# A sequence DFT with odd rows folded once more and even rows sorted by s mod 8

## The chip, the cores and the metric

The kernel runs on one core of a Trainium2 chip. The metric is device time in microseconds, as the median of several runs. TensorE (PE) multiplies matrices into PSUM banks, VectorE (DVE) and ScalarE (ACT) work on SBUF and PSUM, GpSimd (POOL) works on SBUF and issues gathers, and SyncE (SP) issues most of the plain loads and stores. Each engine takes its instructions in the order of the program.

## The reference

What is computed is a Fourier mixing of 8 batches of 3008 x 256 numbers, of which the real part is kept, followed by two dense layers with an ELU between them:

```python
X = np.fft.fft(x, axis=1)
X = np.fft.fft(X, axis=2)
x = X.real.astype(np.float32).reshape(8 * 3008, 256)
h = x @ w_in                        # 256 -> 2048
g = np.where(h > 0.0, h, np.exp(np.minimum(h, 0.0)) - 1.0)
return (g @ w_out).astype(np.float32)   # 2048 -> 256
```

## The kernel before

All matrices are float32. The channel DFT is folded into the first weights once (`fold_chunk`: `Wc` and `Ws` are w_in behind a cosine and a sine transform), so that the sequence DFT of a batch needs only a cosine part R and a sine part I, each of 128 rows (channels) and 1504 + 1 wave numbers; k and 3008 - k share them. `Rr`, `Ir` and `Rb` are rings of 2048 columns (`RING`), which hold R, I and one spread-out row, the transform of channel 128, for all 8 batches one after another. A tile is 256 columns (`TW`), and 47 tiles of 8 slots, each of two blocks of 128 of the 2048 inner channels, give 376 slots.

A slot, by its names in the schedule: P (`mm_P`, Wc x Rr into a PSUM bank `H`), V (`even_part`, adds the spread row to it, gives `E`), Q (`mm_Q`, adds Ws x Ir to `H`), h (`h_minus`, 2E - H, the mirrored wave numbers), b+ and b- (ReLU of the negative on ScalarE), x+ and x- (exponentials), g+ and g- (the ELU, VectorE, into `G`). From tile 2 on the second layer runs as a Winograd product, with four block sums per slot on POOL (`sum_1`, `sum_3`, `sum_2`, `sum_4`) and seven products (X1, X2, X3) on TensorE; `comb_*` and `turn_*` (tiles u, v, ot) put the result together on VectorE, and SP stores it. There are three banks `H`, shared with the DFTs.

The sequence DFT of a batch. `load_x` brings 4 tiles `xl0` to `xl3` of 128 x 6 rows: rows s of the first quarter, and their mirrors 3008 - s, 1504 - s and 1504 + s. Six rows stand on a partition p: rows 4p to 4p + 3 and 508 + 2p + m. Tiles 0 and 3 come by plain DMAs on SP (`ahead`), tiles 1 and 2, whose rows run backwards, by gathers on POOL (`back`) with row numbers from `row_tables`. `fold_x` folds the channels (`e`, `o`) and then the mirrored rows, so that four tiles of 6 x 128 columns remain: EO0 to EO3, for R and I, even and odd wave numbers (`kodd`). In the first batch VectorE folds (the hand-written list `FRONT`, whose times order the program at the start), in later ones POOL does, a piece per slot.

Each of the four transforms (`Dft`) has three products for even rows and three for odd rows (`dft_parts`, called through `dft_mms` and `Dft.mms`, recorded at line 430), with a folded tile as the stationary matrix and a cosine or sine table `MC[ri, kodd]` as the moving one. The even half gives symmetric and antisymmetric columns: ScalarE copies one part (`copy`, tile `anti`), VectorE adds and subtracts (`unfold`, tile `bs`); `plus` and `minus` then join even and odd rows and write k and its mirror into the ring. The times of later transforms are given by `at_dft`: matmuls at 4.75 in a slot, copy, unfold and join in the next one. `T = 4.8` is the unit of the schedule; events are sorted by time, which is the order of the program, and each engine follows it as its operands come. `load_ext`, `get_ext`, `fold_ext`, `dft_ext`, `ext_*` do the same for channel 128 of batches 1 to 7; `x_even` and `dft_ext_0` for batch 0.

Of the kernel before, what the change touches and what calls it, by code (L numbers as in the profile page):

```python
# [9 lines left out]
FP = mybir.dt.float32  # L10
# [17 lines left out]
NH = 189  # L28
BE = 4 * NH
BW = BE + 3 * NE  # L30
# [3 lines left out]

def _dft_consts():

    p = np.arange(128)[:, None]
    out = np.zeros((128, 4, BW), np.float64)
    for ri in range(2):
        fn = np.cos if ri == 0 else np.sin
        for kodd in range(2):
            mat = out[:, 2 * ri + kodd]
            n, h = (NO, NO // 2) if kodd else (NE, NH)

            def block(m, n):  # L50
                k = 2 * np.arange(n)[None, :] + kodd
                s = 4 * p + m if m < 4 else 508 + 2 * p + m
                w = np.where(s == 0, 0.5, 1.0) * (s <= RUN)
                w = np.where(s == RUN, 0.5 if ri == kodd else 0.0, w)
                return s, w * fn(2.0 * np.pi * ((s * k) % SEQ) / SEQ)

            for m in (0, 2, 4):
                s, v = block(m, h)
                anti = (s % 4 == 2) != ri
                if not kodd:  # L60
                    v[:, h - 1] *= ~anti[:, 0]
                if m < 4:
                    c = 0 if m == 2 * ri else h
                    mat[:, c : c + h] = v
                else:
                    mat[:, 2 * h : 3 * h] = v * ~anti
                    mat[:, 3 * h : 4 * h] = v * anti
            for t in range(3):
                mat[:, BE + t * NE : BE + t * NE + n] = block(2 * t + 1, n)[1]
    return out.reshape(128, -1).astype(np.float32)  # L70
# [34 lines left out]

@with_exitstack
def kernel(
# [31 lines left out]
    def xrows(b, row, step, n, rows=6):  # L139

        return bass.AP(
            tensor=xt,
            offset=x.offset + (b * SEQ + row) * ND,
            ap=[[step * ND, n], [1, rows * ND]],
        )
# [3 lines left out]
    ix = cpool.tile([128, 3], I32, tag="ix")  # L149

    def row_tables():

        for c, n, base, step in (
            (0, 128, HALF - 3, -4),
            (1, 128, HALF - 513, -2),
            (2, 128, HALF - 3, -4),
            (2, 1, HALF - 4, 0),
# [3 lines left out]
                    ix[0:n, c : c + 1],  # L163
                    pattern=[[0, 1]],
                    base=base,
                    channel_multiplier=step,
                )
            )

    def load_x(b):  # L170
# [6 lines left out]
        def back(j, few):  # L177
            cols = slice(0, 2 * ND) if few else slice(2 * ND, 6 * ND)
            c = 1 if few else 2 if j == 1 and b == NB - 1 else 0
            pin(  # L180
                nc.gpsimd.indirect_dma_start(
                    out=L[j][:, cols],
# [5 lines left out]
                    element_offset=(b * SEQ + (HALF if j == 1 else 0)) * ND,  # L188
                )
            )  # L190
            if b == NB - 1 and j == 1 and not few:
                nc.gpsimd.dma_start(
                    out=L[1][0:1, 2 * ND : 5 * ND], in_=xrows(b, SEQ - 3, 1, 1, 3)
                )

        def ahead(j, row):
            nc.sync.dma_start(out=L[j][:, 0 : 4 * ND], in_=xrows(b, row, 4, 128, 4))
            nc.sync.dma_start(
                out=L[j][:, 4 * ND :], in_=xrows(b, row + 512, 2, 128, 2)
            )  # L200

        loads = [lambda n=n: back(2 - n // 2, n % 2) for n in range(4)]
        return L, loads + [lambda: ahead(3, HALF), lambda: ahead(0, 0)]


# [186 lines left out]
    for kodd in range(2):  # L392
        for ri in range(2):
            MC[ri, kodd] = cpool.tile(
                [128, BW], FP, tag=f"MC{ri}{kodd}", name=f"MC{ri}{kodd}"
            )

    def load_mats(ri, kodd, cuts=()):
        n = (2 * ri + kodd) * BW
        ends = (0, *cuts, BW)  # L400
# [120 lines left out]
    def fold_x(L, engine_of, cuts_of):  # L521
# [45 lines left out]
        return [E[1], E[3], O[1], O[3]], ops  # L567
# [961 lines left out]
```

## Time and profile before

| | |
|---|---|
| median of 3 runs | 1944.76 us (1944.68 to 1945.83) |
| span of the profiled execution | 1943.2 us |
| instructions in it | 26993 |
| matmul passes on TensorE | 8912 |
| granted TensorE clock | 1.000 |
| SP queue's DMAs, share of 16 engines | 14.8% |

The profile comes from one execution; its span is the time from the first to the last instruction, and the median is 1.6 us above it. In lines of instructions, `H<-MC,o` reads: the tile written, then the tiles read; line numbers are those of the listing, and L430, L436, L439, L442 and L527 are helpers that record all matmuls, the VectorE and POOL sums, the ScalarE operations and the folds. A float32 product appears as two passes.

### The profile page before, as it was taken

The page shows a single profiled execution, that of the slowest core. Times are in us where ns is not written, and L with a number is a line of the kernel's source. Part 1 is how long each engine was busy: PE and PEld are TensorE (multiplying, and loading weights), DVE is VectorE, ACT ScalarE, POOL GpSimd, SP SyncE. Part 2 cuts the span into 40 slices and gives each one's busy share as a digit, 9 for nine tenths or more (in the row PEclk, how much of TensorE's full clock was granted, in tenths as well). Part 3 has the DMA queues.
Part 4 walks back from the last instruction along what each step waited for, and adds up shares of the span by engine and source line. Part 5 has one row for each costly group of instructions (what it writes and reads, how often), then busy time and mean ns, then how long its engine had stood idle before and what let it go on. Part 6 is the DMA issues. An engine that isn't in the chain of part 4 may idle for free.

```text
span 1943.2 us, 26993 instructions
## 1 busy us (share of the span) xinstructions
PE 1933.4 (99%) x8912; PEld 1653.4 (85%) x8912; DVE 1293.2 (67%) x2398; ACT 865.6 (45%) x1671; POOL 1377.6 (71%) x1816
## 2 busy tenths in 40 slices
PE   9999999999999999999999999999999999999999
PEld 6788788888888888888888888888888888888887
DVE  8866666666666666666667666676666766667666
ACT  5644434443444444444444443444434444344443
POOL 4788758876677767787677876777767776556655
PEclk9999999999999999999999999999999999999999
DMA  8145111101112020020210202012020110100101
GB/s 333 44 35 52 34 44 19 49 15 33 33 20 49 12 50 21 18 50 11 54 23 13 52 8 58 12 20 60 7 52 11 20 23 14 17 12 11 23 11 23
DMA packets 263291, 70.25 MB, mean 36 GB/s; under 512 B 248607, under 2 KB 249523, under 8 KB 263153
## 3 DMA queue, kind: packets, MB, share of 16 engines
q1 hardware_dynamic: 257360, 55.69, 14.8%
q0 software_dynamic: 3616, 12.59, 2.1%
q8 instruction: 70, 1.15, 0.2%
q14 instruction: 69, 0.56, 0.1%
q10 hardware_dynamic: 2176, 0.26, 0.1%
HBM read 43.66 MB, written 24.80 MB: 35 GB/s over the span
## 4 chain that ended last, share of the span: by engine, by line
PE 94%; DVE 2%; POOL 2%; ACT 1%; DMA 1%; issue 1%; DVEq 0%; POOLq 0%
PE H L430 38%; PE pB L430 16%; PE pC L430 16%; PE pD L430 16%; PE pA L430 8%; DMA xl<-in_x_dram,ix 1%; POOL WT L439 1%; POOL G L439 1%; DVE G L869 0%; DVE E L839 0%; DVE e L527 0%; POOL w L439 0%; DVE v L436 0%; ACT G L442 0%; DVE pow L310 0%
## 5 line engine op out<-in xcount | busy, mean ns | idle before, releaser
L439 POOL TENSOR_TENSOR G<-G 128x256 f32<-128x256 f32 x1440 | 1036.8, 730 | 508.5 <-DVE G L869 338.6
L839 DVE SCALAR_TENSOR_TENSOR E<-Rb,wex,H 128x256 f32<-128x256 f32 x752 | 327.7, 477 | 544.7 <-PE H L430 541.1
L442 ACT ACTIVATE G<-H 128x512 f32<-128x512 f32 x376 | 224.6, 597 | 960.1 <-DVE G L853 955.4
L430 PE MATMUL H<-Ir,Ws 128*128 128x256 f32 x1504 | 386.9, 380 | 2.0 <-DVE E L839 2.0
L430 PE MATMUL H<-Rr,Wc 128*128 128x256 f32 x1504 | 387.0, 380 | 0.8 <-DVE Ir L436 0.8
L430 PE MATMUL pC<-G,WT 128*128 128x256 f32 x1440 | 369.5, 379 | 0.0
L430 PEld LDWEIGHTS H<-Rr,Wc 128*128 128x128 f32 x1504 | 284.6, 190 | 56.0 <-issue 2.2
L430 PEld LDWEIGHTS H<-Ir,Ws 128*128 128x128 f32 x1504 | 278.8, 189 | 49.6 <-DVE E L839 4.3
L430 PEld LDWEIGHTS pC<-G,WT 128*128 128x128 f32 x1440 | 273.6, 190 | 37.2
L853 DVE SCALAR_TENSOR_TENSOR G<-E,H 128x512 f32<-128x512 f32 x376 | 256.8, 683 | 44.2 <-POOL G L439 5.0
L869 DVE SCALAR_TENSOR_TENSOR G<-G,H 128x512 f32<-128x512 f32 x376 | 255.8, 680 | 43.0 <-ACT G L442 43.0
L869 DVE SCALAR_TENSOR_TENSOR G<-M,G 128x512 f32<-128x512 f32 x376 | 256.7, 683 | 0.4 <-ACT M L442 0.4
L442 ACT ACTIVATE G<-G 128x512 f32<-128x512 f32 x376 | 233.2, 620 | 0.0
L430 PE MATMUL pD<-G,w 128*128 128x256 f32 x784 | 229.4, 379 | 0.5 <-POOL G L439 0.5
L430 PE MATMUL pA<-G,w 128*128 128x256 f32 x784 | 229.3, 379 | 0.0
L430 PE MATMUL pB<-G,w 128*128 128x256 f32 x784 | 229.3, 379 | 0.0
L442 ACT ACTIVATE M<-G 128x512 f32<-128x512 f32 x376 | 224.0, 596 | 3.1 <-DVE G L853 3.1
L442 ACT ACTIVATE M<-M 128x512 f32<-128x512 f32 x376 | 221.0, 588 | 0.1
L430 PE MATMUL pB<-G,WT 128*128 128x256 f32 x720 | 214.8, 380 | 0.3
L430 PE MATMUL pD<-G,WT 128*128 128x256 f32 x720 | 214.1, 379 | 0.0
L430 PEld LDWEIGHTS pD<-G,w 128*128 128x128 f32 x784 | 148.9, 190 | 21.1 <-POOL G L439 0.9
L430 PEld LDWEIGHTS pA<-G,w 128*128 128x128 f32 x784 | 149.0, 190 | 20.5
(148 smaller groups left out, 1408.2 us busy)
## 6 DMA issues: line engine op xcount, KB each, us to landing
out_dram<-ot SPq DMA_DIRECT2D x496, 32.0 KB
xl<-in_x_dram SPq DMA_DIRECT2D x16, 512.0 KB
xl<-in_x_dram SPq DMA_DIRECT2D x16, 256.0 KB
out_dram<-ot SPq DMA_DIRECT2D x256, 2.0 KB
Rb<-r SPq DMA_DIRECT2D x10, 376.0 KB
raw<-in_moe_w_in_dram SPq DMA_DIRECT2D x7, 512.0 KB
MC<-dft_mats SPq DMA_DIRECT2D x3, 943.5 KB
raw<-in_moe_w_out_dram SPq DMA_DIRECT2D x4, 512.0 KB
```

Source lines behind the costliest of these rows:

```text
L430: nc.tensor.matmul(out_, lhsT=lhsT, rhs=rhs, start=start, stop=stop, skip_group_check=True)
L439: pin(nc.gpsimd.tensor_tensor(out=o, in0=a, in1=b, op=op))
L442: pin(nc.scalar.activation(out=o, in_=i, func=func, **kw))
L839: nc.vector.scalar_tensor_tensor(out=S.E[:, c], in0=Rb[:, cols(i)], scalar=wex[:, f : f + 1], in1=S.H[:, c], op0=ALU.mult, op1=ALU.add,)
L853: nc.vector.scalar_tensor_tensor(out=two(S.G[:, 0:512])[:, :, ::-1], in0=two(S.E), scalar=2.0, in1=two(S.H), op0=ALU.mult, op1=ALU.subtract,)
L869: nc.vector.scalar_tensor_tensor(out=o, in0=e, scalar=-1.0, in1=h, op0=ALU.add, op1=ALU.max)
```

## The change

Odd rows of even wave numbers: since a row s and its mirror 752 - s have the same cosine up to the sign that k / 2 decides, the sum S and the difference D of two of the three odd-row column groups are formed once per batch (S0, D0 from EO0; S2, D2 from EO2), and wave numbers 4j and 4j + 2 take only one of them each. Even rows: they are ordered so that a column group has only s = 0 mod 8, s = 4 mod 8 or s = 2 mod 4, and a product runs over a quarter (95 or 94) or a half (189 or 188) of the wave numbers. The tables have 1417 columns for even and 1786 for odd wave numbers, instead of 1887 each.

In return `unfold` has four operations instead of two, joins of even wave numbers go in two halves with a step of two columns, and the rows of `x` need another order: pairs of rows with steps of 8. Each of the 4 tiles is now loaded in 3 pairs, 6 of the 12 pairs by gathers (one each) and 6 by two plain DMAs each. At the start the six gathers and the plain loads of tile 3 (SP) come first, then those of tiles 2, 0 and 1 on the ACT queue, ahead of ScalarE's table load; `w1_chunks[0].load()` on SP comes behind tile 3. The element-wise loads of channel 128 are cut accordingly, into 24 steps. In later batches the six gathers are spread over the same time as the four before.

```diff
-NH = 189
-BE = 4 * NH
-BW = BE + 3 * NE
+NA = (95, 94)
+NC = (189, 188)
+BW = (1417, 1786)
+OFF = (0, 1417, 3203, 4620)
...
+RUNS = (
+    (0, 0, 96, 0, 8),
+    (0, 96, 128, 500, 8),
+    (1, 0, 94, 750, -8),
+    (1, 94, 128, 266, -8),
+    (2, 0, 64, 4, 8),
+    (2, 64, 128, 258, 8),
+)
...
+        def gather(j, pair):
+            back = j in (1, 2)
+            cut = b == NB - 1 and j == 1 and pair == 0
+            c = 3 if cut else pair
+            block = 2 - pair if back else pair
...
+        def runs(j, queue=nc.sync):
+            back = j in (1, 2)
+            for pair, p, q, r, step in RUNS:
+                if back != (pair == 1):
+                    continue
+                row = (0, SEQ, HALF, HALF)[j] + (-r - 1 if back else r)
+                queue.dma_start(
+                    out=L[j][p:q, 2 * pair * ND : (2 * pair + 2) * ND],
+                    in_=xrows(b, row, 8, q - p),
+                )
+
+        loads = [
+            lambda j=j, pair=pair: gather(j, pair)
+            for j, pair in ((3, 1), (2, 0), (2, 2), (0, 1), (1, 0), (1, 2))
+        ]
+        loads += [lambda j=j, **kw: runs(j, **kw) for j in (3, 2, 0, 1)]
...
+        for n, t in ((0, E[1]), (2, O[1])):
+            d = spool.tile([128, 256], FP, tag=f"sd{n}", bufs=1, name=f"sd{n}")
+            sd.append(d)
+            for m, f in ((0, ALU.add), (1, ALU.subtract)):
+                op(f"{'SD'[m]}{n}", d[:, 128 * m : 128 * m + 128],
+                    t[:, 128:256], t[:, 384:512], f)
...
-        if par:
-            n = NO if kodd else NE
-            return [(2 * t + 1, BE + t * NE, n, 0) for t in range(3)]
-        h = NO // 2 if kodd else NH
-        return [(2 * ri, 0, h, 0), (2 - 2 * ri, h, h, h), (4, 2 * h, 2 * h, 0)]
+        na, nc_ = NA[kodd], NC[kodd]
+        if not par:
+            return [
+                (0, 0, 2 * na, 0),
+                (2, 2 * na, nc_, 2 * na),
+                (4, 2 * na + nc_, na + nc_, na),
+            ]
+        z = 3 * na + 2 * nc_
+        if kodd:
+            return [(2 * t + 1, z + t * NO, NO, 0) for t in range(3)]
+        n = (188, 189) if ri else (189, 188)
+        return [
+            (6, z, n[0], 189 if ri else 0),
+            (7, z + n[0], n[1], 0 if ri else 189),
+            (5, z + NE, NE, 0),
+        ]
...
-        h, m = (n + 1) // 2, n // 2
-        tt(o[0:M, 0:h], sym[0:M, 0:h], anti[0:M, 0:h], ALU.add)
-        tt(o[0:M, n - 1 : n - 1 - m : -1], sym[0:M, 0:m], anti[0:M, 0:m], ALU.subtract)
+        tt(ab[:, 0:na], a, b, ALU.add)
+        p, q = (b, a) if ri else (a, b)
+        tt(ab[:, steps_of(nc_ - 1, 94, -1)], p[:, 0:94], q[:, 0:94], ALU.subtract)
+        tt(es[0:M, 0:nc_], ab[:, 0:nc_], c, ALU.add)
+        p, q = (c, ab) if ri else (ab, c)
+        tt(es[0:M, steps_of(n - 1, 188, -1)], p[:, 0:188], q[:, 0:188], ALU.subtract)
...
-    exp_neg(warm)
-    L_first, loads = load_x(0)
-    for load in loads[:5]:
-        load()
+    L_first, loads = load_x(0)
+    for load in loads[:7]:
+        load()
+    for load in loads[7:]:
+        load(queue=nc.scalar)
+    exp_neg(warm)
     w1_chunks[0].load()
-    loads[5]()
...
-        (-8.58, "E0 Ws0 EO0"),
+        (-8.58, "E0 Ws0 EO0 S0 D0"),
-        (-5.76, "w1b EO2"),
+        (-5.76, "w1b EO2 S2 D2"),
-        (24.53, "u2p w4R Xa3 V5 b-4 u3l"),
+        (24.53, "u2p w4R Xa3 V5 b-4 u3l L4"),
-        (32.25, "u3s L3 Q6 w4P g-5 Xb4 b+6 h6 J-up u3M"),
+        (32.25, "u3s L3 L5 Q6 w4P g-5 Xb4 b+6 h6 J-up u3M"),
...
-    for n in range(16):
-        j, k = divmod(n, 4)
+    for n in range(24):
         at(
-            (14.4 + 0.5 * n) * T,
-            lambda j=j, k=k: load_ext(j, 192 * k, 192 * (k + 1)),
+            (14.4 + 0.33 * n) * T,
+            lambda n=n: load_ext(*divmod(n, 6)),
         )
...
-        for n in range(6):
-            t = l0 + gap * n if n < 4 else l0
+        for n in range(10):
+            t = l0 + gap * n / 1.5 if n < 6 else l0
```

`ab`, a new tile of 189 columns, holds the inner sum of `unfold`; `near` takes the place of `anti`, with 95 columns. Each `load_ext` step is two DMAs, one for each row of a pair.

## The prediction

> **What bounds the kernel now.** I read the page first (busy times, chain), then the busy times by stage, then TensorE and VectorE in order of time around two transforms in the middle, then the first 30 us.
>
> ```profile
> PE 1933.4 (99%) x8912; PEld 1653.4 (85%) x8912; DVE 1293.2 (67%) x2398; ACT 865.6 (45%) x1671; POOL 1377.6 (71%) x1816
> ...
> PE 94%; DVE 2%; POOL 2%; ACT 1%; DMA 1%; issue 1%; DVEq 0%; POOLq 0%
> ```
>
> TensorE is busy for 99% and is 94% of the chain. A busy TensorE need not be at its peak, so its pace has to be read from starts (start, length, engine, operation, count):
>
> ```profile
> 702.55 2.07 PE L430 MATMUL H<-MC,o 128*128 128x377 f32 x6
> 704.46 1.03 PE L430 MATMUL H<-Rr,Wc 128*128 128x256 f32 x4
> ...
> 714.82 1.43 PE L430 MATMUL H<-MC,e 128*128 128x188 f32 x6
> 716.08 1.03 PE L430 MATMUL H<-Rr,Wc 128*128 128x256 f32 x4
> ```
>
> Each fp32 product is two passes. An odd-row half of 3 x 377 = 1131 columns takes 704.46 - 702.55 = 1.91 us; an even-row half of 188 + 188 + 376 = 752 takes 1.26 us. Both give 1.68 ns a column with nothing in between: the passes of 188 columns keep the pace of those of 377, although a weight load shows as 190 ns. So a column taken away is 1.68 ns of the span wherever TensorE is fed without a break. It is, by the busy times of the stage after the start (stretch, length, then busy us of PE, PEld, DVE, ACT, POOL, clock, DMA share, GB/s):
>
> ```profile
> 250.00:1700.00 1450.00, 1449.30 (x6640) 1252.32 (x6640) 950.15 (x1772) 631.43 (x1217) 1054.25 (x1391) 1.00 0.14 29
> ```
>
> VectorE in the same window, with the idle time before an instruction and its releaser in brackets:
>
> ```profile
> 705.52 0.87 DVE L839 SCALAR_TENSOR_TENSOR E<-Rb,wex,H 128x256 f32<-128x256 f32 x2 [2.20 <-PE H L430]
> ...
> 717.15 0.87 DVE L839 SCALAR_TENSOR_TENSOR E<-Rb,wex,H 128x256 f32<-128x256 f32 x2 [2.49 <-PE H L430]
> 717.94 0.61 DVE L436 TENSOR_TENSOR bs<-H,anti 128x188 f32<-128x188 f32 x2
> ```
>
> VectorE usually waits 1 to 3 us for the `H` behind each `E`; that is its cover. `E` itself is tight: it ends at 718.02 and the second matmul group of the slot, which reads its bank, starts at 718.24.
>
> The start is another matter; all engines in order of time:
>
> ```profile
> 3.17 0.97 POOL L181 DMA_INDIRECT xl<-in_x_dram,ix  x1 [0.30 <-issue]
> ...
> 5.13 0.96 DVE L527 TENSOR_TENSOR e<-xl 128x768 f32<-128x768 f32 x1 [4.04 <-DMA xl<-in_x_dram]
> ...
> 10.74 0.42 DVE L527 TENSOR_TENSOR e<-xl 128x256 f32<-128x256 f32 x1 [0.46 <-DMA xl<-in_x_dram,ix]
> ...
> 25.39 0.53 DVE L436 TENSOR_TENSOR Rr<-bs,pB 128x377 f32<-128x377 f32 x1
> ...
> 26.21 1.02 PE L430 MATMUL H<-Rr,Wc 128*128 128x256 f32 x4
> ```
>
> From 5.13 to 25.92 VectorE is a chain with one gap of 0.46 us; it begins when a plain load of `xl3` lands and ends 0.3 us before the first product P0 at 26.21. A gather takes 7.6 us from issue (3.17) to its reader (10.74). The DMA engines are full from 4 us on (shares 0.95 and above).
>
> **What the Trainium skill says.** (1) DMA: Bandwidth & Descriptors, "Anatomy of one DMA — SWDGE (gpsimd) path", prices a gather at 2.0 us plus its bytes at 436 GB/s, 2.6 us for 256 KB; the trace has 7.6 to 8 us in the full engines of the start, so the page serves as the lower end only. (2) The same page, "Queues, rings and completion order": each DMA engine goes round the queues that have work, so a third queue (ACT's) takes from the share of the gathers. The trace before has no ACT loads; untested. (3) TensorE: Matmul & The Clock Gate, Part 1, "What's actually happening": after about 3.4 us idle the clock falls to half until TensorE has been busy as long. The trace shows 1.000 throughout, as the 46 warm-up matmuls reach to 13.2 us. (4) VectorE: DVE Perf Modes, "The TRN2 errata": an fp32 tensor_tensor lasts (N + 151) / 0.96 ns, 353 ns for 188 where the trace has 343; back to back they start 0.26 us apart (0.61 us for two).
>
> **The change, part by part.**
>
> **Columns.** kodd = 0: 756 + 1131 = 1887 becomes 663 + 754 = 1417; kodd = 1: 752 + 1128 = 1880 becomes 658 + 1128 = 1786. A batch has two of each: 1128 fewer, with as many matmuls. After P0: batches 1 to 7, 7 x 1128 x 1.68 ns = 13.3 us; odd wave numbers of batch 0, 188 columns, 0.3; the channel-128 transforms, 564 and 94 columns, 1.1. Together 14.7 us. The 940 + 470 columns ahead of P0 (2.4 us) are worth nothing, because P0 waits for VectorE (next part).
>
> **Start.** `e3` now needs four plain loads and a gather. POOL issues nine row tables instead of four (0.12 us each), so the first gather goes out near 2.3 us instead of 1.74. Bounds on its landing: 2.3 + 1.1 + 2.6 = 6.0 by the page, 2.3 + 8 = 10.3 by the trace. It is half the size of the first gather before, but three queues share the engines; I take 9.0, so the chain starts 3.9 us later. At 26.21 the old 0.46 us gap and 0.3 us of slack come off: 3.1. The fourth gather, for `e0`, goes out near 6.1 and lands near 13.7, when VectorE gets there (9.60 + 3.9): no further wait. The sixth (8.7 + 8 = 16.7) is needed at 19. VectorE gains ahead of P0: S0, D0, S2, D2 at 0.2 us and the hand-over between dependent ones (0.95 in all), two small sums (0.25), two unfolds at +0.45 (two operations of 95 columns at 0.17 and 0.1 for the dependence), two joins in halves (+0.12 each): 2.3 us. So P0 is 5.4 us late (2.4 and 6.7 at the bounds). Until the first Q, four more such edits (I-sum and three joins, 0.8 us) lie in a VectorE that is 90% busy from 30 to 60 us: +0.9. TensorE is idle for 3 to 4 us at 13 us, so the clock may fall: +0.6 (0 to 2). Start in all +6.9 us (3 to 10). The ACT queue issues eight loads at 0.45 us, done by 4.5 us; its first operand comes later, so this costs nothing.
>
> **Unfold and join, later.** 28 unfolds at +0.45 us, 14 joins of kodd = 0 at +0.12. In 19 of the 28 the next `E` has 0.4 to 1.7 us of idle time before it, so nothing is lost. In 9 a `u` or `v` follows without idle time; less the 0.2 us between `E` and the matmuls, 9 x 0.25 = 2.3 us (0 to 4.5). What queues behind the unfold is G+, G- and h; POOL's sums, which wait for G, are due about 1 us later, so they hold. The copy of `near` on ACT is shorter: nothing.
>
> **POOL.** S0, D0, S2, D2: 128 columns last 0.46 us there, 1.84 us a batch in two slots. A slot with a fold has 4.75 - 3.03 - 1.18 = 0.55 us free; the overrun of 0.37 us is taken by the next slot and is under the 1.5 us between the last sum (806.8) and its reader (808.3). Two more gathers a batch at 1.0 us fall in slots without folds, but partly between the sums: 0.5 us in all (0 to 3). In batch 1 POOL is itself in the chain from 114 to 132 us, and `e0` now waits for a gather issued just before it; some 3 us of idle time at 70 us cover most: +0.8 (0 to 3).
>
> **Channel 128.** 24 steps of two element-wise loads replace 17 loads on SP, as many elements: SP is full from 110 to 181 us and the 31 extra issues at 0.35 us make it 11 us later. Their reader is at 207 us and the stores have two buffers of eight slots: hidden. The unfold and rows of 8 partitions on VectorE (0.65 us each at 219 us) have no idle time around them; five more short operations: +1.5 us (0.5 to 3). SP's twelve `xl` loads a batch instead of four run eight slots ahead: nothing.
>
> **Sum.** -14.7 + 6.9 + 2.3 + 0.5 + 0.8 + 1.5 = -2.7 us against the span of 1943.2; the median 1944.76 is 1.6 above the span. Forecast 1942 us.
>
> **The rivals.**
>
> A, forecast: the start gives most back. 1942, its own range 1938 to 1948. For it: the VectorE chain from 5 to 26 us without gaps. Against: landing times in full engines are a guess.
>
> B: the first gather is quick and the unfolds hide. Landing at 6.5 us and no fall of the clock make the start +3.5; unfolds 1, POOL 0.5, channel 128 0.7: -9.0, 1936 us. For it: the lone gather at 39 us landed in 4.7 us. Against: the engines are full here, at 39 us they are not.
>
> C: slower, because `xl` arrives by gathers one after another. The place is VectorE's wait for `e0` below 25 us, whose pair comes with the fourth gather. If the first lands at 10.3 and each next 3.5 us later, the fourth is there at 20.8: `e0` is 11.2 us late, the sixth at 27.8 makes `e1` another 1.0 late, and with -0.8 + 2.3 + 0.9 + 2.0 as above the start costs 16.6: 1944.8 - 14.7 + 16.6 + 5.1 = 1952 us. It decides from a start of 9.6 us on (14.7 less the other 5.1), a fourth landing near 15. For it: gathers moved about 155 GB/s before (1.5 MB from 4 to 13.6 us), and 3.5 us for 256 KB is half of that, with one queue more. Against: as many bytes have to come, and the loads behind them on SP are issued no earlier.
>
> D: fewer columns don't save time, because short passes wait for their weights; then nothing of the 14.7 is left and A becomes 1956. The 188-column halves at full pace speak against it: the shortest new parts are 188 to 190 columns. It goes with C.
>
> **How the numbers follow.** A 0.37, B 0.31, C with D 0.32. 0.2% is 3.9 us, about what can be told from no change here: below 1940.9 is faster, above 1948.6 slower. A lies mostly inside (0.06 faster, 0.28 same, 0.03 slower), B is faster but for 0.01, C is slower but for 0.02. So faster 0.36, same 0.31, slower 0.33. Since both signs hold most of the chance, A's own range stands above; for 8 in 10 I go from 1933 (-14.7 + 3 + 0.5: every unknown at its lower bound) to 1956 (C).
>
> **What would show it.** Halves of 1417 columns at 1.68 ns; P0 near 31.6 us; the first `e` of VectorE near 9 us behind a gather; `E` waits of TensorE at about nine unfolds; TensorE still at 99% from 250 to 1700 us, in a stretch 13 us shorter. The forecast is wrong if P0 comes before 29 or after 35 us, if TensorE stalls at most unfolds, or if POOL's sums hold it.

## The result, and the profile after

The changed kernel takes 1977.77 us (median of 4 runs, 1974.57 to 1980.33) beside 1945.3 us for the kernel before on the same chip: a ratio of 1.0165, 95% interval 1.0151 to 1.0179. It is slower by 32.5 us, where 1942 was forecast. The profiled execution took 1980.33 us with a span of 1978.5, 35.3 us above the span before.

Busy times and the chain of waits, from the page of the changed kernel:

```profile
PE 1935.5 (98%) x8912; PEld 1656.1 (84%) x8912; DVE 1316.0 (67%) x2517; ACT 862.6 (44%) x1671; POOL 1403.5 (71%) x1869
...
PE 88%; DVE 4%; DMA 3%; POOL 2%; SPq 1%; issue 1%; ACT 0%; ACTq 0%; DVEq 0%; POOLq 0%
```

TensorE's share of the chain fell from 94% to 88%, and DMA, SP's queue and POOL came in: time is lost in waits, not in work. Its busy time is no smaller than before although 8 x 1128 = 9024 columns are gone; part of it was spent at half clock, at the start and behind four later waits (both below). (In this kernel the helpers recorded as L430, L436 and L527 before are L475, L481 and L572, and most variants have them two lines further on.)

The product halves themselves, in TensorE's order of time (start, length):

```profile
734.23 0.81 PE L475 MATMUL H<-MC,sd 128*128 128x188 f32 x4
734.87 0.80 PE L475 MATMUL H<-MC,o 128*128 128x377 f32 x2
735.50 1.03 PE L475 MATMUL H<-Rr,Wc 128*128 128x256 f32 x4
...
745.86 1.27 PE L475 MATMUL H<-MC,e 128*128 128x188 f32 x6
746.97 1.03 PE L475 MATMUL H<-Rr,Wc 128*128 128x256 f32 x4
```

The odd half of 754 columns takes 735.50 - 734.23 = 1.27 us, the even half shown, of 658 (`kodd` = 1), takes 1.11: 1.68 to 1.69 ns a column, as before. The change does what it says; rival D is out. The loss has to be elsewhere, and the quickest way to it is the start of each slot's P product (a mark that every kernel has) against the same mark in the kernel before. The lag in us, worked out from the two traces, at the slots between which it changes:

| slot (time before) | after | stage that ends here |
|---|---|---|
| 0 (26.2) | 16.9 | start, up to P0 |
| 8 (73.6) | 22.7 | rest of the hand-written start |
| 31 (197.3) | 21.5 | slots that build batch 1's folds |
| 45 (276.0) | 32.2 | transform of channel 128 |
| 276 (1436.2) | 30.9 | batches 2 to 6 |
| 288 (1497.2) | 36.8 | last batch's gathers |
| 375 (1925.4) | 35.1 | last transform |

There are three rises: the start (22.7), slots 31 to 45 (10.7) and slot 278 (5.8 between the two marks of the table). And there is a stretch, slots 45 to 276, with the transforms of batches 2 to 5 and all but the last half-transform of batch 6, in which 5546 columns, 9.3 us, went and 1.3 us were gained.

**The start.** Stretches of 2 us in the changed kernel (stretch, length, busy us of PE, PEld, DVE, ACT, POOL, clock, DMA share, GB/s):

```profile
16.00:18.00 2.00, 0.00 (x0) 0.00 (x0) 0.67 (x2) 0.00 (x0) 0.00 (x0) 0.50 0.17 54
18.00:20.00 2.00, 0.00 (x0) 0.00 (x0) 0.79 (x2) 0.00 (x0) 0.00 (x0) 0.50 0.21 78
20.00:22.00 2.00, 0.00 (x0) 0.00 (x0) 0.00 (x0) 1.69 (x3) 0.00 (x0) 0.50 0.21 76
```

From 16 us TensorE and POOL stand still and VectorE nearly, and so do the DMA engines: a share of 0.17 to 0.21, where it was 1.01 to 1.09 at these times before. One of these stretches in the kernel before:

```profile
18.00:20.00 2.00, 1.78 (x9) 1.24 (x8) 1.97 (x3) 0.37 (x2) 0.00 (x0) 1.00 1.09 426
```

A wait for DMAs while the DMA engines are idle is not a lack of bandwidth. VectorE and ScalarE in order of time, with what they wait for:

```profile
11.59 0.96 DVE L572 TENSOR_TENSOR e<-xl 128x768 f32<-128x768 f32 x1 [10.23 <-DMA xl<-in_x_dram]
...
17.33 0.43 DVE L301 TENSOR_SCALAR pow<-raw 128x512 int32<-128x512 int32 x1 [3.91 <-DMA raw<-in_moe_w_in_dram]
...
22.44 0.69 DVE L355 SCALAR_TENSOR_TENSOR pow<-raw,pow 128x512 int32<-128x512 int32 x1 [3.62 <-ACT pow L487]
```

```profile
0.75 19.52 ACTq L238 DMA_DIRECT2D xl<-in_x_dram  x8
20.30 1.28 ACT L487 ACT_TABLE_LOAD   x1 [20.30 <-DMA xl<-in_x_dram]
```

The first fold waits for a plain load, not for the gather (which landed at 11.2 us itself, 2.2 us later than forecast). The eight loads on ACT's queue take 19.52 us to issue instead of 4; ScalarE's first real work, of which VectorE waits for the result, stands behind them.

**Channel 128.** SP's queue, then POOL, then TensorE:

```profile
206.09 23.43 SPq L1191 DMA_DIRECT2D out_dram<-ot  x48
229.56 0.43 SPq L837 DMA_DIRECT2D xs<-xe_dr  x1
```

```profile
231.87 0.38 POOL L484 TENSOR_TENSOR xs<-xs 128x96 f32<-128x96 f32 x1 [5.15 <-DMA xs<-xe_dr]
```

```profile
232.67 3.81 PE L475 MATMUL H<-MC,xe 128*8 128x190 f32 x24 [4.19 <-POOL xe L484]
```

The last load of the scattered tile stands on SP behind 48 stores that the element-wise loads had held up, and TensorE waits 4.19 us for it. The kernel before has the same 48 stores, but there they came just behind that load:

```profile
181.01 0.59 SPq L716 DMA_DIRECT2D xs<-xe_dr  x1
181.70 24.60 SPq L1070 DMA_DIRECT2D out_dram<-ot  x48
```

In the changed kernel, then, the order of the two on SP is turned round. Behind its wait for `xe` TensorE waits three more times for `E`, up to 2.35 us, because VectorE has the 8-row operations ahead of it.

**Gathers between sums.** POOL, then TensorE, in the middle:

```profile
514.71 0.73 POOL L484 TENSOR_TENSOR G<-G 128x256 f32<-128x256 f32 x1 [2.72 <-DVE G L990]
515.58 0.96 POOL L217 DMA_INDIRECT xl<-in_x_dram,ix  x1
516.56 2.35 POOL L484 TENSOR_TENSOR G<-G 128x256 f32<-128x256 f32 x3
```

```profile
518.15 0.70 PE L475 MATMUL pB<-G,WT 128*128 128x256 f32 x2 [0.47 <-POOL G L484]
```

Spaced at two thirds of a slot, some gathers stand behind the first sum of a slot and ahead of the sums for which TensorE waits next. In the last batch one tile's gather is cut, and its second part, a plain DMA on POOL, waits for the first to land:

```profile
1475.61 0.55 POOL L228 DMA_DIRECT2D xl<-in_x_dram  x1 [2.95 <-DMA xl<-in_x_dram,ix]
```

TensorE's wait for the sums queued behind it is 3.97 us, ending at 1477.78:

```profile
1477.78 1.22 PE L475 MATMUL pB<-G,WT 128*128 128x256 f32 x2 [3.97 <-POOL G L484]
```

**Half clock behind the waits.** A wait of TensorE can cost more than its length. Stretches behind the two longest, columns as above:

```profile
234.00:237.00 3.00, 3.00 (x11) 0.78 (x5) 0.00 (x0) 0.00 (x0) 2.84 (x4) 0.50 0.64 180
1477.00:1482.00 5.00, 4.22 (x10) 3.42 (x11) 0.69 (x1) 0.48 (x1) 4.61 (x6) 0.50 0.20 58
```

TensorE is back at work and runs at 0.50. The clock fell at four waits behind slot 0, of 2.01 us (ending at 89.37 us), 4.19 (232.67), 2.35 (257.81) and 3.97 (1477.78). Each time it stayed down for 3.4 us, the last time for 6.8. In these times TensorE was busy for 15.2 us; half of that, 7.6 us, is an estimate of what the clock took beyond the waits themselves: 1.7 us at slot 8, 3.3 of the rise between slots 31 and 45, 2.6 of that at slot 278. In the kernel before, the clock is at 1.00 throughout.

### The profile page after: what moved, and what is told of

Same layout as the page of the kernel before. It is cut to its first block, busy times and chain, and to the rows that moved or that the text cites. A ratio compares the mean times of both kernels' runs of the same rounds, so it can differ in the third digit from the quotient of the medians.

```text
span 1978.5 us, 27318 instructions
## 1 busy us (share of the span) xinstructions
PE 1935.5 (98%) x8912; PEld 1656.1 (84%) x8912; DVE 1316.0 (67%) x2517; ACT 862.6 (44%) x1671; POOL 1403.5 (71%) x1869
## 4 chain that ended last, share of the span: by engine, by line
PE 88%; DVE 4%; DMA 3%; POOL 2%; SPq 1%; issue 1%; ACT 0%; ACTq 0%; DVEq 0%; POOLq 0%
PE H L475 35%; PE pC L475 15%; PE pB L475 15%; PE pD L475 15%; PE pA L475 8%; DMA xl<-in_x_dram 2%; POOL G L484 2%; SPq L1191 1%; DVE G L990 1%; DVE E L960 1%; POOL xl L217 0%; DVE bs L481 0%; DVE v L481 0%; DMA wx<-Ws 0%; DVE u L481 0%
## 5 line engine op out<-in xcount | busy, mean ns | idle before, releaser
L475 PE MATMUL H<-Ir,Ws 128*128 128x256 f32 x1504 | 389.4, 381 | 5.6 <-DVE E L960 4.7
L475 PE MATMUL H<-Rr,Wc 128*128 128x256 f32 x1504 | 387.5, 380 | 3.0 <-DVE Ir L481 2.0
L475 PE MATMUL pC<-G,WT 128*128 128x256 f32 x1440 | 371.1, 380 | 0.0
L475 PEld LDWEIGHTS H<-Rr,Wc 128*128 128x128 f32 x1504 | 284.8, 190 | 54.5 <-issue 5.3
L475 PEld LDWEIGHTS H<-Ir,Ws 128*128 128x128 f32 x1504 | 279.2, 190 | 56.0 <-DVE E L960 9.3
L475 PEld LDWEIGHTS pC<-G,WT 128*128 128x128 f32 x1440 | 274.8, 191 | 37.7
L475 PE MATMUL pA<-G,w 128*128 128x256 f32 x784 | 229.3, 379 | 0.0
L475 PE MATMUL pB<-G,w 128*128 128x256 f32 x784 | 229.3, 379 | 0.0
L475 PE MATMUL pD<-G,w 128*128 128x256 f32 x784 | 229.3, 379 | 0.0
L475 PE MATMUL pB<-G,WT 128*128 128x256 f32 x720 | 216.8, 383 | 10.0 <-POOL G L484 9.7
L475 PE MATMUL pD<-G,WT 128*128 128x256 f32 x720 | 214.6, 380 | 0.0
L475 PEld LDWEIGHTS pD<-G,w 128*128 128x128 f32 x784 | 149.1, 190 | 20.3
L475 PEld LDWEIGHTS pA<-G,w 128*128 128x128 f32 x784 | 148.9, 190 | 20.5
```

What stands on the lines that cost most here:

```text
L475: nc.tensor.matmul(out_, lhsT=lhsT, rhs=rhs, start=start, stop=stop, skip_group_check=True)
```

## The experiments

Each variant is compared with the kernel before, timed beside it on the same chip. The lags are those of the table above, from each variant's profiled execution. e1, f3, f4 and g1 run the same program up to P0, and their lags there are 7.2 to 8.1 us, so a difference of 1 us between two single executions is not to be read. Later stages vary more: the runs of e1, f3 and f5 spread over 6 to 11 us, those of g1 over 2.5.

| | median, us | ratio to before (95%) | slot 0 | 8 | 31 | 45 | 276 | 288 | 375 |
|---|---|---|---|---|---|---|---|---|---|
| after | 1977.77 | 1.0165 (1.0151 to 1.0179) | 16.9 | 22.7 | 21.5 | 32.2 | 30.9 | 36.8 | 35.1 |
| e1_sixteen | 1964.82 | 1.0104 (1.0087 to 1.0121) | 7.2 | 8.6 | 7.7 | 14.1 | 12.8 | 18.6 | 17.0 |
| e2_spq | 1982.24 | 1.0189 (1.0158 to 1.0220) | 13.3 | 22.6 | 21.8 | 33.5 | 32.2 | 38.2 | 36.6 |
| f6_spq | 1966.73 | 1.0108 (1.0091 to 1.0125) | 6.8 | 8.3 | 7.4 | 20.4 | 19.1 | 24.8 | 23.2 |
| b1_94_34 | 1964.66 | 1.0098 (1.0081 to 1.0115) | 11.6 | 19.3 | 19.3 | 19.3 | 19.3 | 19.4 | 19.4 |
| b2_96_32 | 1948.12 | 1.0015 (1.0009 to 1.0022) | 2.3 | 2.5 | 2.5 | 2.5 | 2.5 | 2.7 | 2.7 |
| f3_gap | 1951.41 | 1.0031 (1.0021 to 1.0040) | 7.6 | 9.1 | 8.2 | 18.3 | 11.3 | 10.7 | 9.0 |
| f4_ext | 1961.83 | 1.0085 (1.0068 to 1.0102) | 7.7 | 9.1 | 8.8 | 13.3 | 12.0 | 18.4 | 16.7 |
| f5_gap_ext_order | 1949.85 | 1.0025 (1.0017 to 1.0033) | 6.4 | 10.1 | 12.6 | 17.0 | 10.0 | 9.3 | 7.7 |
| g1_late | 1944.10 | 0.9994 (0.9985 to 1.0002) | 8.1 | 8.1 | 7.4 | 8.0 | 1.2 | 0.6 | -1.1 |
| g3_w0sp | 1943.50 | 0.9990 (0.9984 to 0.9997) | 7.4 | 7.4 | 6.7 | 8.4 | 1.5 | 0.9 | -0.8 |
| h1_e0first | 1941.98 | 0.9981 (0.9974 to 0.9989) | 5.4 | 6.0 | 5.3 | 5.9 | -0.9 | -1.6 | -3.2 |
| h2_lateweights | 1943.54 | 0.9992 (0.9985 to 0.9999) | 5.3 | 6.7 | 6.0 | 6.7 | -0.2 | -0.9 | -2.5 |

### How many DMA engines a load can use: e1, e2, b1, b2, f6

A page of the Trainium skill that the prediction had open has the clue in another place. DMA: Bandwidth & Descriptors, "Why a DMA increments its semaphore by 16 and not by 1", says that a DMA is spread over the largest number of engines, up to 16, that divides the outermost dimension of both of its sides, and that plain DMAs with a smaller number take the lowest-numbered engines. Two of the new runs of rows have 94 and 34 partitions, which are 2 x 47 and 2 x 17: two engines, and the same two each time. 96 and 32 are multiples of 16. The trace agrees with the number: at 21 to 22 us of the changed kernel the share was 0.13, two engines of sixteen, at 49 GB/s. Which engines they are, no run here shows.

e1 cuts the mirrored runs at 96 partitions, with as many loads and bytes:

```diff
+                if back and (j, b) != (1, NB - 1):
+                    q, p, r = (96, p, r) if p == 0 else (q, 96, 250)
                 row = (0, SEQ, HALF, HALF)[j] + (-r - 1 if back else r)
```

> The changed kernel, but the plain loads of the pair whose rows run backwards are cut in 96 and 32 partitions instead of 94 and 34 (in the last batch tile 1 keeps 94 and 34; the two partitions that thereby get other rows have zero weights). Theory 1, the loads of 94 and 34 partitions run on two of the sixteen DMA engines: the stretch of about 50 GB/s from 22 to 30 us is gone, the ACT queue's eighth load goes out before 14 us instead of 20.3, P0 comes near 34 us instead of 43.15 and the time falls by 8 to 12 us. Theory 2, it is the ACT queue and the limit of loads in flight: with as many loads P0 stays within 2 us of 43. Theory 3, the gathers set the start: P0 stays as well.

e2 leaves the runs at 94 and 34 and puts all loads on SP, the table load first on ACT, so that ScalarE waits behind no load:

```diff
+    exp_neg(warm)
     for load in loads[:7]:
         load()
+    w1_chunks[0].load()
     for load in loads[7:]:
-        load(queue=nc.scalar)
-    exp_neg(warm)
-    w1_chunks[0].load()
+        load()
```

> The changed kernel, but all plain loads of x at the start are issued by SP, those of tiles 2, 0 and 1 behind the first weight chunk, and ScalarE's table load stands first. The 94 and 34 remain. Theory 1 (two engines): tile 1's loads of 94 and 34 are still late, so the sums xa and x-even wait to beyond 20 us, but the wait of VectorE for ScalarE's first power (3.6 us) goes: P0 36 to 40 us, 3 to 7 us gained. Theory 2 (ACT queue held up): P0 falls to 31 to 33 us, as the forecast had it. Theory 3 (gathers): no change.

f6 is both edits together, the fourth corner of a square.

> e1_sixteen with all plain loads on SP and the table load first on ACT, the fourth corner of the square with the changed kernel (1977.8), e1_sixteen (1964.8) and e2_spq (1982.2). Theory, the number of DMA engines that a load of 94 or 34 partitions can use is the start's cause: with 96 and 32 the queue makes little difference, 1962 to 1967. Rival, the two causes act together and ACT's queue blocks ScalarE for eight loads: 1958 to 1961, P0's lag down from 7.2 by 3 us or more. Counter-rival, one queue is slower than two: 1968 to 1972, as with e2_spq.

The square is 1977.8 and 1964.8 us with ACT's queue (94/34, then 96/32), 1982.2 and 1966.7 with SP alone. The cut is worth 13.0 us on one queue and 15.5 on the other; the queue is worth nothing, against the expectation of e2. There P0 came 3.6 us earlier but slot 8 did not: at 68.21 us VectorE waited 6.35 us for a small load, `wex`, and TensorE 4.78 for VectorE (the same wait is shown for b1, below). ScalarE standing behind its loads is a symptom: with 96 and 32 partitions the same eight issues on ACT end at 8.3 us. At slot 8 the lag falls from 22.7 to 8.6. The same stretches as above, in e1, the first and the last:

```profile
16.00:18.00 2.00, 0.00 (x0) 0.00 (x0) 2.00 (x4) 0.31 (x2) 0.00 (x0) 1.00 1.03 384
...
20.00:22.00 2.00, 1.24 (x5) 1.25 (x6) 1.93 (x9) 0.00 (x0) 0.00 (x0) 0.75 1.09 417
```

The DMA engines are full again and VectorE works without a break from 16 us. The waits that are left are for gathers: that of the first fold, at 8.60, was in the forecast; the 1.98 us for `e0`, at 15.16, was not, and it is where rival C looked.

The size is measured alone in the kernel before, where nothing else of the change is present. Its two-row loads of tiles 3 and 0, 128 partitions each, are cut in two:

```diff
-            nc.sync.dma_start(
-                out=L[j][:, 4 * ND :], in_=xrows(b, row + 512, 2, 128, 2)
-            )
+            for p, q in ((0, 94), (94, 128)):
+                nc.sync.dma_start(
+                    out=L[j][p:q, 4 * ND :],
+                    in_=xrows(b, row + 512 + 2 * p, 2, q - p, 2),
+                )
```

This is b1; b2 has 96 in both places of 94.

> The kernel before, with the loads of two rows per partition of tiles 3 and 0 cut in 94 and 34 partitions. Theory 1: the first fold, at 5.13 us before, waits for a load on two engines, 188 KB at some 25 GB/s each plus their share of everything else: 9 us or later, and P0 (26.21 before) 3 to 8 us later. Theory 2 and 3: P0 within 1 us of the next run's.

> The same, cut in 96 and 32 partitions, so with as many loads and bytes. Theory 1: within 1 us of the kernel before, as only the count of loads is different (12 in flight at the start instead of 10, two issues of 0.45 us). If the limit of eight loads in flight matters by itself, the first weight chunks come later here too, and P0 is 1 to 3 us late.

With as many loads in both, 94/34 costs 1964.66 - 1948.12 = 16.5 us more than 96/32, all of it before slot 8: by the lags 9.3 us up to P0, more than the 3 to 8 expected, and 7.5 more up to slot 8. The first fold of VectorE, in b1 and then in b2:

```profile
14.96 0.96 DVE L529 TENSOR_TENSOR e<-xl 128x768 f32<-128x768 f32 x1 [13.87 <-DMA xl<-in_x_dram]
```

```profile
5.41 0.96 DVE L529 TENSOR_TENSOR e<-xl 128x768 f32<-128x768 f32 x1 [4.32 <-DMA xl<-in_x_dram]
```

The second part belongs to batch 1, whose loads SP issues in b1 from 43.35 us on. SP's queue and VectorE, in b1:

```profile
64.61 0.39 SPq L484 DMA_DIRECT2D wex<-wx  x1
67.13 0.87 DVE L841 SCALAR_TENSOR_TENSOR E<-Rb,wex,H 128x256 f32<-128x256 f32 x2 [8.37 <-DMA wex<-wx]
```

`wex` brings 1 KB that another DMA of 1 KB, `wx`, has to write first. `wx` was issued at 54.22 us, and it took until 64.61 before `wex` could follow; in the kernel before that took 2.3 us (42.75 to 45.06). From 56 to 64 us the DMA share was 0.13 to 0.21. That the small write stood behind batch 1's loads on the same engines fits this, but no run shows it alone.

The remaining 2.9 us of b2 against the kernel before (1945.27 in that job) come with two more loads: the first weights land later, and VectorE waits 2.10 us for `raw` at 9.34. Although every batch has these loads, the lag of b1 stands from slot 8 on (19.3 to 19.4): issued slots ahead of their readers, the later ones have time.

### Where POOL's gathers stand: f3

e1 with one token changed, the gathers of later batches a slot apart as before the change:

```diff
-            t = l0 + gap * n / 1.5 if n < 6 else l0
+            t = l0 + gap * n if n < 6 else l0
```

> e1_sixteen with the gathers of batches 1 to 7 due at the beginning of a slot again, as before the change, rather than at two thirds of a gather's spacing, between two block sums of POOL. Nothing else differs; compared with e1_sixteen (1964.8 us). Theory, gathers between sums stall TensorE: 1.2 us a batch in six batches (from slot 45 to slot 276 the lag changed by less, since the removed columns pay for it) and the 5.8 us at slot 280, where a DMA of POOL waits for a landing; 6 to 13 us go, 1952 to 1958, and the lag of the P products behind the kernel before falls between slots 45 and 276 rather than standing at 13 to 14. Rival, the unfolds on VectorE cost what the columns save: no stall belongs to a gather, 1962 us or more and a lag that stands. What would leave only the 5.8 us: about 1959, with a lag that falls at slot 280 alone.

f3 takes 1951.41 us, 13.4 less than e1 and just below the 1952 to 1958 expected. From slot 45 to 276 the lag falls by 7.0 us (e1: 1.3), and from 276 to 288 it falls by 0.6 instead of rising by 5.8. Together 12.1 us for the position of six gathers a batch, some 2.6 of them the half clock behind the wait at slot 278, which e1 has as well. (At slot 375 the two executions are only 8.0 us apart, since that of f3, at 1955.01 us, lost 3.7 us more between slots 31 and 45.) POOL in f3 at a gather of the same batch:

```profile
512.19 2.23 POOL L486 TENSOR_TENSOR G<-G 128x256 f32<-128x256 f32 x3 [3.28 <-DVE G L992]
514.57 0.96 POOL L217 DMA_INDIRECT xl<-in_x_dram,ix  x1
515.55 0.74 POOL L486 TENSOR_TENSOR G<-G 128x256 f32<-128x256 f32 x1
```

The gather is as long as before (0.96 us) and still between sums. But it stands ahead of the fourth only, which is needed last; in the changed kernel it stood ahead of three.

### Channel 128: f4, f5, g1

f4 is e1 with the loads of `xs` on ACT's queue:

```diff
-                nc.sync.dma_start(
+                nc.scalar.dma_start(
                     out=xs[:, j], in_=xe_dr[j].rearrange("b (p m) -> p b m", m=6)
```

> e1_sixteen with the loads of the scattered channel-128 tile (xs from xe_dr) issued by ACT's queue rather than SP's, where the last of them stood behind 48 stores. Compared with e1_sixteen, where the lag of the P products rises by 5.6 us from slot 31 to slot 37. Theory, the position on SP: POOL's wait of 5.15 us and TensorE's of 4.19 us at 232 us go, and the rise falls to 2 to 3.5 us; what is left is VectorE's operations on 8 rows. Total 1962 to 1963. Rival, VectorE's operations on 8 rows are all of it: the rise stays within 1 us of 5.6. Counter-rival: ACT's issues hold up its own exponentials, and the rise grows.

TensorE's wait for `xe` is gone, and the rise from slot 31 to 45 is 4.5 us, where e1 has 6.3, f3 10.1 and f6 13.0. The same code on SP costs a different amount in each execution: the last `xs` load stands behind 48 stores in all of them, but TensorE's wait for `xe` was 1.39 us in e1, 4.92 in f3 and 6.41 in f6, and the clock fell behind the longer ones. So the 3.0 us gained against e1, which had the shortest of these waits, may understate it. The rise up to slot 37 is 3.8 us, where 2 to 3.5 was expected. What remains are mainly waits for `E`, up to 2.35 us, behind VectorE's 8-row operations. But the edit made a wait of its own. ACT in f5, which has the same edit:

```profile
138.34 0.60 ACT L489 ACTIVATE G<-H 128x512 f32<-128x512 f32 x1 [9.54 <-DMA xe_dr<-x]
```

The first `xs` load had moved up in the program to slot 20, and all of ScalarE waited 9.54 us behind it until the element-wise loads were written; TensorE lost 3.7 us of that at 141 us (in f4 the wait was 6.38 us, and TensorE lost 0.5).

f5 has the edits of f3 and f4, and the gathers in another order:

```diff
-            for j, pair in ((3, 1), (2, 0), (2, 2), (0, 1), (1, 0), (1, 2))
+            for j, pair in ((3, 1), (0, 1), (2, 2), (2, 0), (1, 0), (1, 2))
```

> Both edits above on e1_sixteen, and the six first gathers in the order in which VectorE needs them: tile 3's, then tile 0's (plain on the other side), 2, 2, 1, 1, i.e. the pair for e0 comes second rather than fourth. Theory: the sum of the two parts, and the 1.98 us for which e0 waited for the fourth gather; P0's lag falls from 7.2 to 5 to 6 us, total 1944 to 1954, about level with the kernel before. Rival, the gathers land at the pace of full DMA engines in whatever order: P0's lag stays within 1 us of 7.2, because e2 then waits instead.

1949.85 us, within the expectation but only 1.6 below f3. P0's lag is 6.4, short of the 5 to 6 expected and inside the rival's range: 1.2 us less than in f3 and 0.7 less than in e1, so hardly more than executions differ. The waits above took back what it gave. One more came in between slots 5 and 8. TensorE waited 2.02 us for `Ir` at 76.81, and then ran at half clock; that stretch in f5, columns as above:

```profile
78.15:81.56 3.41, 3.41 (x9) 2.66 (x9) 2.47 (x5) 0.00 (x0) 1.71 (x2) 0.50 0.00 0
```

g1 is f3 with all three of these mended: the `xs` loads on ACT held to slot 31, the 8-row operations moved later, into idle time of VectorE, and the join that TensorE waited for at 77 us moved ahead of the weight operations of VectorE. (The copies of channel 128 have a third buffer, so that ScalarE doesn't wait for the later joins.)

```diff
-    at(30.0 * T, get_ext)
+    at(31 * T, get_ext)
...
-    at(35 * T + 1.5, lambda: ext_rows(0, vtt))
+    at(35 * T + 4.3, lambda: ext_rows(0, vtt))
...
-    at(36 * T + 0.2, lambda: ext_unfold(1, vtt))
-    at(36 * T + 1.5, lambda: ext_rows(1, vtt))
+    at(36 * T + 4.4, lambda: ext_unfold(1, vtt))
+    at(36 * T + 4.5, lambda: ext_rows(1, vtt))
...
-        (32.25, "u3s L3 L5 Q6 w4P g-5 Xb4 b+6 h6 J-up u3M"),
-        (33.32, "b-6 J-down"),
+        (32.25, "u3s L3 L5 Q6 w4P g-5 Xb4 b+6 h6 J-up J-down u3M"),
+        (33.32, "b-6"),
```

> e1_sixteen with the gathers at the beginning of a slot (as f3_gap, 1951.4 us) and three further moves. The loads of the scattered channel-128 tile are on ACT's queue, but held to their place in the program, at slot 31, after all element-wise loads; in f4_ext and f5 the first of them had moved up to slot 20, where ACT waited 6.4 and 9.5 us for it. The joins of 8 rows on VectorE are moved back by 2.8 units (first part) and the second unfold and join by 4.2 and 3, into idle time of VectorE. The second join of batch 0's I for odd wave numbers is ahead of three weight operations of VectorE, behind which TensorE waited 1.4 us at 77 us in f3. Theory, these waits are the loss of channel 128 and of slot 8: the lag of the P products rises by under 1.5 us from slot 31 to 45 (f3: 10), slot 8 is 1.5 us earlier than in f3 (9.05), and the total is 1940 to 1945, at or below the kernel before (1945.2). Rival, VectorE's extra operations take the time wherever they stand: the rise from slot 31 to 45 stays over 3 us, total 1946 to 1950.

1944.10 us, inside the expected range and the same as the kernel before. The rise from slot 31 to 45 is 0.7 us (f3: 10.1) and the lag doesn't grow from slot 0 to slot 8 (f3: by 1.5). So the 8-row operations, as many as in f3, cost nearly nothing where VectorE has idle time; four waits of TensorE for `E` are left, 0.31 to 1.26 us (two before the change), and behind P0 the clock no longer falls. What each of the three moves gave is not parted. The window in the middle, in g1, has TensorE as full as before the change:

```profile
250.00:1700.00 1450.00, 1449.13 (x6683) 1257.78 (x6683) 967.27 (x1866) 633.78 (x1226) 1078.88 (x1434) 1.00 0.14 29
```

It has 1449.13 of 1450 us (the changed kernel 1437.67), with 6683 passes instead of 6640 before the change: shorter ones, so more of them in the same time.

### What is left of the start: g3, h1, h2

g3 is g1 with the first chunk of weights loaded first, its VectorE operations ahead of the first fold, and all plain loads on SP:

```diff
+    w1_chunks[0].load()
+    exp_neg(warm)
-    for load in loads[:7]:
-        load()
-    for load in loads[7:]:
-        load(queue=nc.scalar)
-    exp_neg(warm)
-    w1_chunks[0].load()
+    for load in loads:
+        load()
...
-        (-20.84, "e3 o3"),
-        (-19.11, "w0a w0b w0p w0R c3"),
-        (-17.62, "w0s w0M"),
+        (-22.0, "w0a w0b w0p w0R w0s w0M"),
+        (-20.84, "e3 o3 c3"),
```

> g1_late with the first chunk of weights loaded first on SP, ahead of the plain loads of x, its six operations of VectorE (2.9 us) ahead of the first fold, in the time in which VectorE waits for the first gather, and all plain loads on SP, so that ScalarE is free for its part of them. Theory: P0 comes 2 to 3 us earlier than in g1_late, and the total falls by as much, to 1938 to 1943. Rival, the loads are the limit, not VectorE: the weights' 256 KB come ahead of those of x, the folds start later by what is gained, and the total is within 1 us of g1_late.

P0 came only 0.8 us earlier, and the total is 0.6 us below g1: that is the rival's case (within 1 us). VectorE in g3:

```profile
15.38 1.03 DVE L574 TENSOR_TENSOR e<-xl 128x512 f32<-128x512 f32 x2 [5.06 <-DMA xl<-in_x_dram,ix]
```

The time saved goes into a wait of 5.06 us for the fourth gather. That is rival C's mechanism, at its place: `e0` can start at 15.38 us, in e1 at 15.16. So h1 takes tile 0 second, whose gather is then the second of six, and folds it ahead of tile 2:

```diff
-            for j, pair in ((3, 1), (2, 0), (2, 2), (0, 1), (1, 0), (1, 2))
+            for j, pair in ((3, 1), (0, 1), (2, 2), (2, 0), (1, 0), (1, 2))
...
-        (-16.21, "e0a e2b o2"),
-        (-14.32, "e2a o0 c2"),
+        (-16.21, "e0a o0 e0b"),
+        (-14.32, "e2b e2a o2 c2"),
...
-        (-9.8, "e0b c1 o1 c0 x-odd x-copy Wc0"),
+        (-9.8, "c1 o1 c0 x-odd x-copy Wc0"),
```

(Plain loads: tile 0 ahead of tile 2 too.)

> g3_w0sp with tile 0 brought second (its gather second of six, its plain loads ahead of tile 2's), and all of VectorE's folds of tile 0 (e0, o0; 2.2 us) right behind tile 3's, ahead of tile 2's. In g3 VectorE waited 5.06 us for the fourth gather. Theory, the start is set by the landing of the gathers in the order in which VectorE uses them: the second is there by 12 us, 2.2 us of folds move into the wait, P0 comes 1.5 to 2.2 us earlier than in g3 (lag 7.37 to about 5.5), total about 1941.7 (g3: 1943.5). Rival, the gathers' pace is the limit and the last of them is needed as late as before: o2 and x-even then wait instead, P0 within 0.7 us of g3.

VectorE in h1, in the same stretch:

```profile
11.33 0.69 DVE L574 TENSOR_TENSOR e<-xl 128x512 f32<-128x512 f32 x1
...
15.46 0.69 DVE L574 TENSOR_TENSOR e<-xl 128x512 f32<-128x512 f32 x1 [1.84 <-DMA xl<-in_x_dram,ix]
```

The fourth gather is no earlier, but only 1.84 us are waited for it. P0 comes 1.9 us earlier and the total falls to 1941.98 us, 0.9981 of the kernel before (0.9974 to 0.9989): the lowest here, 3.4 us below it.

h2 moves three weight operations from ahead of P0 to behind it:

```diff
-        (-4.55, "w2b R-even u0b w2d u0a EO1 w1d"),
+        (-4.55, "R-even u0a EO1 w1d"),
...
-        (0.82, "R-down O-even Irc I-sum u1l V0"),
+        (0.82, "R-down O-even Irc I-sum u0b w2b w2d u1l V0"),
```

> h1_e0first with three weight operations of VectorE (w2b, u0b, w2d; 1.3 us) moved from ahead of P0 to behind the sum of I. Theory, VectorE's chain up to P0 has no idle time, so P0 comes 1.3 us earlier than in h1; whether it is kept depends on 30 to 60 us, where VectorE is about 90% busy: the lag at slot 5 is 0 to 1.3 us smaller than in h1, total 1940.5 to 1942. Rival, they are late for ScalarE and POOL, and the lag at slot 5 is that of h1 or more.

It gained nothing: P0's lag is 0.1 us smaller, those of slots 5 and 8 0.7 us larger (7.5 and 6.7), and the median is 1.6 us above h1. Ahead of P0 VectorE did come 1.2 us earlier to its operation `pow<-raw` (26.99 us, h1: 28.18), but there it began beside a sum of POOL and lasted 1.51 us instead of 0.42 (last section). At slot 5 the result is the rival's; that the operations are late for ScalarE and POOL, its reason, is not shown.

## Why the prediction was wrong

**Columns: right.** 14.7 us were to go at 1.68 ns a column; the halves take that. From slot 45 to the end, where batches 2 to 7 are transformed, g1 gains 8.0 + 1.1 = 9.1 us; their columns are six times 1.9, that is 11.4.

**Unfolds and joins: inside the range.** TensorE's starts part the missing 2.3 us of that stretch, worked out from the two traces as what each pass starts later than the columns ahead of it need. Products that read POOL's sums started 3.0 us late in all in g1, 1.8 before the change; those that wait for `E` 1.4 us, 0.5 before. So by way of `E` unfolds and joins cost at most 0.9 us in six batches, where 2.3 (0 to 4.5) was forecast for seven; POOL's sums cost 1.2, with 0.5 forecast, and whether gathers or a later `G` held them is not parted.

**Start: the step that failed most.** "Start in all +6.9 us (3 to 10)" became 22.7. The failed sentence is "The ACT queue issues eight loads at 0.45 us, done by 4.5 us; its first operand comes later, so this costs nothing": they were issued until 20.3 us. Every plain load was taken at the pace of a full set of DMA engines, and only gathers were doubted; the partition counts 94 and 34, which stand in the diff, were not read as a number of engines, although the page that says so was cited for two other things. Put right by 96 and 32 alone (e1), the start is 8.6 us with P0 at 33.4, beside 6.9 and 31.6 in the forecast; the wait for the fourth gather that it left out (1.98 us) is about the difference. The mechanism of the sum (VectorE's chain starting later and being longer) was right, and the cost of the cut, 14 us at slot 8, was missing from it. The clock's fall was foreseen at 0.6 us; with TensorE idle from 13.2 us the changed kernel ran at 0.50 from 15.2 to 35.7 us, as TensorE: Matmul & The Clock Gate, Part 1, "What's actually happening", of the Trainium skill has it for idle stretches, but P0 waited for VectorE then, so it was little of the loss. For falls behind later waits, some 7.6 us by the estimate above, the forecast had no term.

**POOL's gathers: a term mis-sized by an order.** "Two more gathers a batch at 1.0 us fall in slots without folds, but partly between the sums: 0.5 us in all (0 to 3)" failed: their position cost 12.1 us (e1 against f3), 5.7 over the middle batches and 6.4 at the last one's cut gather. The place was named; what wasn't asked is ahead of which sum each gather stands, and that a DMA on POOL that waits for a landing stops the sums behind it.

**Channel 128: mis-sized, and one wait missed.** "The 31 extra issues at 0.35 us make it 11 us later. Their reader is at 207 us and the stores have two buffers of eight slots: hidden" failed: the last load that TensorE needs came behind the 48 stores on SP instead of ahead of them (a wait of 4.19 us). The 8-row operations were named with 1.5 us for want of idle time. Together the lag rose by 10.7; with both mended, by 0.7.

**Rivals.** The time lies beyond the range given for 8 in 10 (1933 to 1956). C, at 1952 the slower side, had the right sign, the right stage and 16.6 of the start's 22.7 us, but another cause: in the changed kernel the gathers landed 1.3 to 1.6 us apart, not 3.5, and as waits they show only in variants with 96 and 32 partitions, as 2 to 5 us in e1, g3 and h1. B was out with the first fold at 11.59 us. That h1 takes the 1942 us of the forecast is no hit: it has five changes of order that the change under study has not.

**Open.** In the changed kernel ACT's fifth load was issued at 12.6 us and the last at 20.0. In the trace the first plain loads on SP and ACT share eight semaphores in turn, and each from the ninth on waits for the one that it reuses: ACT's fifth for that of ACT's first, a load of 94 partitions, which was complete at 12.58 us. So the slow loads held up those behind them; what more semaphores or fewer loads would give was not tried. The 2.9 us of b2 are another matter: the load of `raw` for which VectorE waits there was issued at 2.15 us (1.68 before), ahead of any such wait, and landed at 9.3 us instead of 6.3; why is not shown. And only 94 with 34 was set against 96 with 32, no other partition counts.

## What to carry to other kernels

Before a load is split, factor the partition counts of the pieces: 96 + 32 and 94 + 34 move the same bytes and differed by 16.5 us, and a wait for DMAs while their share is 0.2 is the sign of it in a profile. An issue or an operation that is added to an engine in the critical loop costs by what stands behind it there, not by its own length: ask ahead of which operand it stands, and whether it waits. To find several losses at once, compare the start of one recurring instruction between two traces, slot by slot: each rise points to a stage, though several causes can lie in it. And when a wait of TensorE of 2 us or more is priced, the clock behind it belongs to the price: in the changed kernel some 7.6 us of 32.5.

## What the runs showed of the hardware that was not expected

- Loads that can use two DMA engines moved 49 GB/s where little else ran (a share of 0.13, two of sixteen engines: the changed kernel from 21 to 22 us, b1 from 60 to 64); loads that fill them all moved 366 to 426 from 16 to 22 us, in e1 and in the kernel before.
- An idle time of about 2 us can be enough for the clock to fall, if not always; the page cited above has about 3.4 us, and these runs have less. Waits of 2.01 us (changed kernel), 2.02 (f5) and 2.37 (e1) were each followed or ended by 3.4 us at 0.50; in h1 1.86 us ahead of 29.72, after a stretch in which TensorE had been idle already, by 0.50 from 31.7 to 35.2 us, so that P0 took 2.01 us instead of 1.13; but 1.92 us in g3 (ending at 31.65) and 2.52 in b2 (15.52) by nothing. The fall can come as late as 2.0 us behind the end of the wait (h1), and every such time that ends within the span is 3.41 us long or a whole multiple of it (6.83 at 1476 us, 20.5 at the start of the changed kernel). Of the 1.9 us that h1 gained at P0 on g3, 1.4 are left at slot 8; more warm-up work for TensorE was not tried.
- The landing of the fourth gather moved little: issued at 6.7 to 6.9 us in the changed kernel and in ten variants of it, it was there at 14.3 to 16.1, whatever queue and order the plain loads had.
- In h2, 17 operations `TENSOR_SCALAR` of VectorE on 512 columns began while POOL was computing, and each ended 0.28 to 0.29 us behind POOL's operation, after 0.41 to 1.52 us; the 15 others took 0.41 to 0.43. The kernel before has the same pattern: 17 of them, up to 1.54 us.
